# A two-branch sequence mixer: hand-ordered emission against a graph placed by a list schedule

## The chip, the cores and the metric

The kernel runs on one core of one Trainium2 chip. The metric is the device time of one execution in microseconds (us); lower is better. Each kernel was run several times on the same chip as the kernel before, and a run counts as slow when it is more than 1.5% above the fastest run of the same kernel.

Engine names: PE is the matmul engine (TensorE) and PEld its weight loads, DVE is VectorE, ACT is ScalarE, POOL is GpSimd, SP is SyncE, which issues nearly all DMAs here.

## The reference, cut to what matters

`x = A_q` is 2048 x 640 in bf16. Branch A is a long causal convolution over the sequence with a short shift convolution ahead of it; branch B is a mixer MLP; a gate per row mixes the two.

```python
def reference(A_q, A_k, A_v, A_shift_k, A_ssm_k, A_ssm_D, B_x, B_w1, B_w2, B_w3, B_w4, gate_w):
    def _A_ref(q, k, v, shift_k, ssm_k, ssm_D):
        # k_shift: 4-tap causal shift convolution of k, per column (cut)
        kv = k_shift * v
        # kv_f, kf_f: rfft of kv and of ssm_k, zero-padded to 2*S (cut)
        y_f = kv_f * kf_f[None, :, :, :]
        # y: irfft of y_f, first S rows, bf16 (cut)
        y = y + kv * ssm_D[None, None, :]
        return q * y
    def _B_ref(x, w1, w2, w3, w4):
        h = _gelu(_layernorm(x, axis=-1) @ w1)
        # hs: four column groups of h shifted by +1, -1, +2, -2 rows, then @ w2 (cut)
        x1 = x + hs
        h2 = _gelu(_layernorm(x1, axis=-1) @ w3) @ w4
        return x1 + h2
    x = A_q
    g = _sigmoid((x * gate_w).sum(-1, keepdims=True))
    # returns g * _A_ref(...) + (1 - g) * _B_ref(...)
```

## The kernel before

Sequence row `s = 16*p + t1` lies on partition `p`, slot `t1`. The Fourier transform is done in two matmul steps with an exchange between them: step 1 multiplies each of 16 slots by a table `F1` (128 x 128), the result is evacuated from PSUM into a stage `GR`, a set of 16 DMAs moves it across partitions (`gx`), step 2 multiplies by a small table `M3`. There are eight such passes: for each half of the columns (`dh`) and each half of the frequencies (`h`), one pass for the filter (`h` pass) and one for `kv`. After a `kv` pass the product with the transformed filter `HH` is multiplied back by `M3` into `VR`. An inverse for each half of the columns loads `VR` across partitions (`vx`) and multiplies by `I1`.

```python
    def gate_slab(s):                    # 16 times: product on DVE, row sum on ACT
        pr = ring.tile([P, D], BF16, name="pr", tag="xy", bufs=3)
        nc.vector.tensor_tensor(out=pr[:], in0=QX[:, s, :], in1=GW[:], op=ALU.mult)
        nc.scalar.activation(out=JK, in_=pr[:], func=ACT.Identity, accum_out=Z[:, s:s + 1])

    def step1(src, dh, h, isH, lag):
        ds = slice(dh * DH, (dh + 1) * DH)
        for tp in range(T1 // 2):
            ps = pst()
            for j in range(2):
                ...                      # F1 matmuls of slot 2*tp+j
            nc.scalar.copy(out=GR[:, 2 * tp:2 * tp + 2, :], in_=ps[:, :, 0:DH])
            yield 0.28, (lag if tp == T1 // 2 - 1 else 0.0)

    def gx_load(kp):
        gx = ring.tile([P, 2, DH], BF16, name="gx", bufs=3)
        for j in range(2):
            exchange(gx[:, j, :], GR, 2 * kp + j)        # one DMA of 80 KB, issued by SP
        return gx

    def h_step2():
        for kp in range(T1 // 2):
            gx = gx_load(kp)
            ...                          # M3 matmuls, ACT writes HH[:, ..., 0, :]
            if kp == 7:                  # HH[:, ..., 1, :] = the two partition halves swapped, 4 DMAs
                ...

    def inv(dh):
        for tp in range(T1 // 2):
            ps = pst()
            vx = ring.tile([P, 2, 2, DH], BF16, name="vx", tag="pv", bufs=3)
            for j in range(2):
                t1 = 2 * tp + j
                nc.sync.dma_start(out=vx[:, j], in_=VR.rearrange("(a r) t h d -> a r t (h d)", a=8)[:, t1])
                ...                      # 2 matmuls with I1
            ...                          # DVE: KV = ps * KV (q was loaded into KV)
            yield 0.56, 0.6

    def conv():
        for dh in range(2):
            for h in range(2):
                if (dh, h) != (0, 0):
                    yield from step1(HT, dh, h, True, LAG)       # filter pass
                    yield from h_step2()
                if (dh, h) == (1, 0):
                    q_half(0)
                    yield from inv(0)
                yield from step1(KV, dh, h, False, LAG)          # kv pass
                yield from x_step2(h, LAG if h else 0.0)
        q_half(1)
        yield from inv(1)
    # ... the front (LN, W1, W2, first filter pass) in written order, then:
    mix(cv, m2, 57.4, 86.0)              # convolution and W3/W4 work interleaved by two estimates
```

Four PSUM buffers serve all of it.

## Time and profile before

| | before |
|---|---|
| median of three runs, us | 375.05 (374.65 to 375.49) |
| span of the profiled run, us | 372.8 |
| PE busy, us; idle, us | 266.4; 106.4 |
| mean granted PE clock | 0.895 |

These are the page's lines on busy time, the span in 40 slices (each digit is the busy share, or for PEclk the granted clock, in tenths), and the chain of work that ended last, all of the kernel before. Names like R_70 are shared buffers: R_70 holds `VR`, GR the stage.

```profile
PE 266.4 (71%) x1594; PEld 151.8 (41%) x1608; DVE 186.1 (50%) x339; ACT 184.3 (49%) x280; POOL 57.0 (15%) x139
PE   0003999784697979998499998679998635634594
DVE  5326999999799985120254113231630002323286
PEclk9999999989699989999789999899999865655589
...
DVE 25%; PE 23%; DMA 22%; ACT 8%; POOL 7%; issue 7%; SPq 7%; DVEq 0%; ACTq 0%
```

No engine is full. PE is the busiest and yet idle for 106 us, so the question is where it waits. The next view sums busy time by stretches of the span of the kernel before; its columns are the stretch, its length, busy time and instruction count of each engine, the granted clock, the DMA share and the GB/s moved.

```profile
core 0: us, PE busy (x) PEld busy (x) DVE busy (x) ACT busy (x) POOL busy (x), PEclk, DMA share, GB/s
0.00:40.00 40.00, 7.56 (x42) 4.16 (x43) 19.82 (x64) 9.47 (x9) 26.98 (x76) 1.00 0.94 325
40.00:112.00 72.00, 59.51 (x431) 37.99 (x433) 68.78 (x140) 53.47 (x98) 22.69 (x56) 0.93 0.19 51
112.00:205.00 93.00, 80.50 (x492) 46.90 (x497) 46.30 (x74) 60.18 (x85) 7.34 (x9) 0.94 0.43 108
...
320.00:350.00 30.00, 12.95 (x45) 4.39 (x42) 9.68 (x12) 3.86 (x6) 0.00 (x0) 0.56 0.38 88
```

Three weak places show: the start (7.6 us of PE work in 40), the front until 112 us, in which DVE is the full engine (68.8 of 72), and the end, where the second inverse runs nearly alone at a clock of 0.56.

The gate costs DVE and ACT this much (the three groups of the kernel before, the second of which reads out the sums of the first; columns: busy us, mean ns):

```profile
L330 ACT ACTIVATE I_75<-pr 128x640 bf16<-128x640 bf16 x16 | 11.8, 735 | 3.1 <-DVE R_78 L297 2.8
L330 ACT ACTIVATION_READ_ACCUMULATOR I_75<-pr 128x1 f32 x16 | 3.0, 188 | 0.0
L329 DVE TENSOR_TENSOR pr<-QX,R_72 128x640 bf16<-128x640 bf16 x16 | 7.5, 486 | 0.4 <-ACT I_75 L330 0.4
```

### The profile page before, as it was taken

How to read it: one execution, taken by the hardware profiler on the slowest of the kernel's cores; microseconds unless marked ns; L12 is line 12 of the kernel's file. 1: busy time of each engine (PE TensorE's matmuls, PEld its weight loads, DVE VectorE, ACT ScalarE, POOL GpSimd, SP SyncE). 2: the span in 40 equal slices, each digit the busy share in tenths (PEclk: the TensorE clock that was granted, in tenths of full speed). 3: DMA queues.
4: the chain of work that ended last, by engine and by line, in shares of the span. 5: the costliest groups of instructions: out<-in, count | busy, mean ns of one | idle time of the engine just before them, and what ended most of it. 6: DMA issues, size and time to landing. Idle time of an engine off the chain costs nothing.

```text
span 372.8 us, 4494 instructions
## 1 busy us (share of the span) xinstructions
PE 266.4 (71%) x1594; PEld 151.8 (41%) x1608; DVE 186.1 (50%) x339; ACT 184.3 (49%) x280; POOL 57.0 (15%) x139
## 2 busy tenths in 40 slices
PE   0003999784697979998499998679998635634594
PEld 0002566353473545663356554235653212301163
DVE  5326999999799985120254113231630002323286
ACT  1133655689888758636367535125577644600000
POOL 3787500013674110000000000000000000000000
PEclk9999999989699989999789999899999865655589
DMA  7997400322046254047830446531402656144424
GB/s 281 409 347 269 138 0 2 127 55 53 7 101 167 56 149 138 15 110 147 206 69 20 104 110 138 130 84 33 103 10 66 142 122 199 34 100 118 117 79 150
DMA packets 47136, 43.87 MB, mean 118 GB/s; under 512 B 2319, under 2 KB 44938, under 8 KB 46986
## 3 DMA queue, kind: packets, MB, share of 16 engines
q1 hardware_dynamic: 47114, 43.59, 43.2%
q8 instruction: 12, 0.20, 0.2%
q14 instruction: 10, 0.08, 0.1%
HBM read 19.99 MB, written 2.62 MB: 61 GB/s over the span
## 4 chain that ended last, share of the span: by engine, by line
DVE 25%; PE 23%; DMA 22%; ACT 8%; POOL 7%; issue 7%; SPq 7%; DVEq 0%; ACTq 0%
DMA gx<-GR 14%; DMA vx<-R_70 6%; PE ps L509 6%; DVE R_72 L372 6%; ACT GR L400 5%; PE ps L496 5%; SPq L456 5%; POOL R_78 L170 4%; DVE R_72 L375 3%; PE ps L440 2%; DVE QX L318 2%; DVE QX L485 2%; SPq L387 2%; PE ps L441 2%; DVE pq L433 2%
## 5 line engine op out<-in xcount | busy, mean ns | idle before, releaser
L496 PE MATMUL ps<-XNT,R_76 128*128 128x512 bf16 x230 | 62.6, 393 | 1.1 <-ACT GR L400 0.3
L509 PE MATMUL ps<-R_72,R_78 128*128 128x320 bf16 x384 | 59.0, 304 | 0.3 <-ACT GR L400 0.2
L433 DVE TENSOR_TENSOR pq<-xs,R_71 128x1280 bf16<-128x1280 bf16 x32 | 26.3, 823 | 58.4 <-ACT xs L431 56.7
L509 PEld LDWEIGHTS <-R_78 128*128 128x128 bf16 x384 | 38.2, 99 | 18.6 <-issue 3.3
L400 ACT CAST GR<-ps 128x640 bf16<-128x640 f32 x64 | 39.4, 725 | 9.4 <-PE ps L397 8.9
L260 PE MATMUL pt<-IDN,xn 128*128 128x128 bf16 x160 | 14.7, 247 | 39.4 <-DVE xn L257 39.2
L500 ACT ACTIVATE R_78<-ps 128x1024 bf16<-128x1024 f32 x24 | 24.8, 1032 | 22.7 <-PE ps L496 22.7
L431 ACT CAST xs<-ps 128x640 bf16<-128x640 f32 x32 | 22.3, 695 | 27.7 <-PE ps L429 27.7
L458 PE MATMUL ps<-vx,I_75 128*128 128x320 bf16 x64 | 18.3, 387 | 23.5 <-DMA vx<-R_70 23.4
L496 PEld LDWEIGHTS <-R_76 128*128 128x128 bf16 x240 | 24.0, 101 | 25.9 <-issue 6.4
L514 DVE SCALAR_TENSOR_TENSOR QX<-ps,OMG,QX 128x640 bf16<-128x640 f32 x16 | 14.1, 883 | 40.9 <-PE ps L509 40.7
L415 ACT ACTIVATE R_71<-ps 128x640 bf16<-128x640 f32 x32 | 22.4, 700 | 23.2 <-PE ps L414 23.1
L461 DVE TENSOR_TENSOR KV<-ps,KV 128x640 bf16<-128x640 f32 x16 | 13.2, 824 | 38.1 <-PE ps L458 38.1
L260 PEld LDWEIGHTS <-xn 128*128 128x128 bf16 x160 | 12.3, 112 | 43.4 <-DVE xn L257 40.0
L429 PE MATMUL ps<-gx,M_103 128*128 128x320 bf16 x64 | 18.0, 349 | 15.5 <-DMA gx<-GR 15.3
L315 PE MATMUL ps<-R_76,R_78 128*128 128x320 bf16 x160 | 26.7, 323 | 2.3 <-issue 2.1
L442 ACT CAST R_70<-ps 128x640 bf16<-128x640 f32 x32 | 22.3, 698 | 9.7 <-PE ps L441 9.6
L257 DVE TENSOR_SCALAR xn<-QX,rs,mb 128x640 bf16<-128x640 bf16 x32 | 13.5, 438 | 26.5 <-PE pt L260 21.1
L277 PE MATMUL ps<-XNT,R_76 128*128 128x512 bf16 x96 | 24.7, 402 | 2.3 <-ACT XNT L265 2.1
L440 PE MATMUL ps<-pq,M_103 128*128 128x320 bf16 x64 | 20.6, 332 | 4.5 <-DVE pq L433 4.0
L414 PE MATMUL ps<-gx,M_103 128*128 128x320 bf16 x64 | 17.2, 304 | 8.9 <-DMA gx<-GR 8.4
L372 DVE TENSOR_TENSOR R_72<-R_70,R_72 128x1280 bf16<-128x1280 bf16 (+3 forms) x32 | 23.2, 750 | 0.0
(113 smaller groups left out, 368.3 us busy)
## 6 DMA issues: line engine op xcount, KB each, us to landing
gx<-GR SPq DMA_DIRECT2D x128, 80.0 KB
R_71<-R_71 SPq DMA_DIRECT2D x16, 320.0 KB
vx<-R_70 SPq DMA_DIRECT2D x32, 160.0 KB
R_71<-in_A_ssm_k_dram SPq DMA_DIRECT2D x5, 512.0 KB
R_70<-in_A_k_dram SPq DMA_DIRECT2D x2, 1280.0 KB
KV<-in_A_v_dram SPq DMA_DIRECT2D x1, 2560.0 KB
KV<-in_A_q_dram SPq DMA_DIRECT2D x2, 1280.0 KB
out_dram<-QX SPq DMA_DIRECT2D x16, 160.0 KB
```

The costliest lines, as they stand in the source:

```text
L260: nc.tensor.transpose(out=pt[:, j, k * P:(k + 1) * P], in_=xn[:, k * P:(k + 1) * P], identity=IDN[:])
L277: nc.tensor.matmul(ps[:, j, :], lhsT=lhsT, rhs=xt[:, k, :], start=(k == 0), stop=(k == DT - 1))
L315: nc.tensor.matmul(ps[:, j, 0:DH], lhsT=gst_ap(k, s), rhs=W2[:, k, j * DH:(j + 1) * DH], start=(k == 0), stop=(k == DT - 1))
L372: nc.vector.tensor_tensor(out=dst[:, a:b], in0=src, in1=cj, op=ALU.mult)
L400: nc.scalar.copy(out=GR[:, 2 * tp:2 * tp + 2, :], in_=ps[:, :, 0:DH])
L415: nc.scalar.activation(out=HH[:, 2 * kp:2 * kp + 2, 0, :], in_=ps[:, :, 0:DH], func=ACT.Copy, scale=1.0 / S)
L431: nc.scalar.copy(out=xs[:], in_=ps[:, :, 0:DH])
L433: nc.vector.tensor_tensor(out=pq[:], in0=xs[:].unsqueeze(2).to_broadcast([P, 2, 2, DH]), in1=HH[:, 2 * i:2 * i + 2], op=ALU.mult)
L440: nc.tensor.matmul(pv[:, j, 0:DH], lhsT=M3[:, 1, :], rhs=pq[:, j, 0, :], start=True, stop=False)
L496: nc.tensor.matmul(ps[:, j, :], lhsT=W3[:, k, (f0 + j) * P:(f0 + j + 1) * P], rhs=xt[:, k, :], start=(k == 0), stop=(k == DT - 1))
L500: nc.scalar.activation(out=GTP[:, (3 * c + f0 // 4) % 5, f0 % 4:f0 % 4 + 2, :], in_=ps[:], func=ACT.Gelu_apprx_tanh)
L509: nc.tensor.matmul(ps[:, j, 0:DH], lhsT=GTP[:, (3 * c + f // 4) % 5, f % 4, i * P:(i + 1) * P], rhs=W4[:, f, j * DH:(j + 1) * DH], start=( ...
```

## The change

The intent is to let a planner decide the order. Every piece of work becomes a node with a cost per engine that may do it, its dependencies, and the buffers it takes and gives. A list schedule simulates the core with these costs, always starting the ready node with the lowest key; the nodes are then emitted in the planned order. Keys come from a table `WANTED` of hand- or search-tuned start and end values for each stage.

```diff
+class Graph:
+    def forward(self):                       # cut to the choice of the next node
+        for opts, q in queues.items():
+            es = [e for e in opts if clock[e] <= now + 1e-9]
+            if opts == "D" and len(dmas) >= 8 and dmas[-8] > now + 1e-9:
+                continue
+            if opts == "AV" and "A" not in es and len(q) + len(queues.get("A", ())) < self.spill:
+                continue                     # an evacuation goes to DVE only if ACT is busy and 2 wait
+            ...                              # lowest key whose buffers are free wins
+        if n.bytes is not None:              # all transfers share one line in the plan
+            line = max(now + 1.9, line) + n.bytes
+            fin = line + 0.7
+    def run(self):
+        for n in sorted(self.nodes, key=lambda n: n.start):
+            n.fn(n.engine)
+SPILL = 2
+WANTED = {
+    "W1.0": (337, 568), "W2": (504, 741.5), "p0.1": (-20, 674), "p0.gx": (115.5, 1589.5),
+    "p3.1": (64, 1032.5), "p4.hh": (770, 1452.5), "inv1": (550.5, 1330.5), "W3.3": (461, 634), ...
+}
@@ convolution @@
-                    yield from step1(HT, dh, h, True, LAG)
-                    yield from h_step2()
-                ...
-                yield from step1(KV, dh, h, False, LAG)
-                yield from x_step2(h, LAG if h else 0.0)
+    def pass1(r):                            # r 0..3 the filter, r 4..7 kv
+        stage = (RA, RB)[r % 2]              # two stages in place of GR
+        war = [k_gx[r - 2, k] for k in range(T1)] if r >= 2 else k_hn_free
+        ...
+            evs.append(evac(2 * DH, PSD, [t], ...))          # ACT, or DVE by the spill rule
+    def pass2(r):
+            if r < 4:                        # filter spectrum to DRAM, 4 writes of 320 KB a pass
+                    k_hd[r, kp // 2] = dma(lambda r=r, kp=kp: HD[r, :, (kp - 1) * 2 * DH:(kp + 1) * 2 * DH], ...)
+    def hh_load(r):                          # ahead of each kv pass: one straight, one swapped copy
+        for half in range(2):
+            ns = [dma(lambda ks=ks: HH[:, 0, ks, :], lambda q=q, fs=fs: HD[q, :, fs]..., P * 5120, 5120, deps)]
+            for a in (0, 64):
+                ns.append(dma(lambda a=a, ks=ks: HH[a:a + 64, 1, ks, :], ..., 64 * 5120, 5120, deps))
@@ gate @@
-        nc.vector.tensor_tensor(out=pr[:], in0=QX[:, s, :], in1=GW[:], op=ALU.mult)
-        nc.scalar.activation(out=JK, in_=pr[:], func=ACT.Identity, accum_out=Z[:, s:s + 1])
+                for i in range(4):           # 80 one-column matmuls on the normalised, transposed x
+                    for k in range(DT):
+                        nc.tensor.matmul(P32(b)[:, 1, i:i + 1], lhsT=XNT[:, xb.slot, k, i * P:(i + 1) * P],
+                                         rhs=GWC[:, k:k + 1], start=(k == 0), stop=(k == DT - 1))
+                nc.vector.tensor_tensor(out=ZN[:, cs], in0=P32(b)[:, 1, 0:4], in1=SD[:, cs], op=ALU.mult)
+                nc.vector.scalar_tensor_tensor(out=Z[:, cs], in0=MV[:, cs, 0], scalar=GS[:], in1=ZN[:, cs], ...)
@@ inverse and end @@
-            nc.vector.tensor_tensor(out=g, in0=ps[:, :, 0:DH], in1=g, op=ALU.mult)
+                    nc.vector.scalar_tensor_tensor(out=g, in0=P32(b)[:, j, 0:DH], scalar=G32[:, t1:t1 + 1], in1=g, ...)
-        nc.vector.scalar_tensor_tensor(out=QX[:, s, :], in0=KV[:, s, :], scalar=G32[:, s:s + 1], in1=QX[:, s, :], ...)
+        k_add.append(dve(2 * D, TWO, ..., lambda p=p: nc.vector.tensor_tensor(
+            out=QX[:, 2 * p:2 * p + 2, :], in0=KV[:, 2 * p:2 * p + 2, :], in1=QX[:, 2 * p:2 * p + 2, :], op=ALU.add)))
```

Not shown: the row-shift copies are made by DMA instead of DVE, and the sine tables are made by POOL, DVE and ACT together instead of mostly by POOL.

## The prediction

> **What bounds it now.** No engine is full: the page gives PE 71%, DVE 50%, ACT 49% of a 372.8 us span. The chain of waits: DVE 25%, PE 23%, DMA 22% (the exchange gx<-GR alone 14%, vx 6%), SP queue 7%. Windows show three parts:
> - 0 to 40 us, PE busy 7.6: POOL makes the sine tables (32 pieces of 0.44 us, chained to DVE and ACT); W1 starts at 35 us.
> - 40 to 280, PE busy about 34 of each 40 us. At 40 to 120 DVE is full (39.8 and 37.0 of 40); from 120 PE leads, interrupted by "step, evacuate (8 x 0.6 us on ACT alone), exchange (16 issues at 0.65 us, then 2.7 us to land), step".
> - 280 to 373: MLP work has run out, the convolution's serial end stays: PE 25.1 of 40, 12.9 of 30, 16.3 of 23. The granted clock falls to 0.73 and 0.56, and 128x320 matmuls take 0.27 us apart instead of 0.135. The Trainium skill (TensorE: Matmul & The Clock Gate, Part 1: The HAM clock gate) says an idle PE falls to half clock; the trace agrees.
>
> PE's own work: 526 thousand columns; eight 128x320 matmuls take 1.09 us in dense stretches, hence about 224 us at full clock, 235 to 245 at the clock of dense stretches (0.91 to 1.00). Some 130 us are start, end and gaps.
>
> **What changes.**
> - *Moved, the main gain:* all four h passes go before the kv passes, into the front where PE waited for DVE; two stages let the next pass's first step overlap an exchange; MLP thirds are spread to the very end, so that inverse 1 (16 vx loads at 1.35 us, PE nearly idle at 326 to 354 now) runs beside some 25 us of W3/W4 work, at a better clock.
> - *Removed:* gate products on DVE (16 x 0.49) and ACT (16 x 0.92): 22 us; shift copies on DVE 5 us; addy (16 x 0.88) becomes 8 adds of 0.81: 7 us. Table work is split over three engines.
> - *Added:* 80 one-column matmuls with weight loads (about 7 us of PE); HD writes 5.2 MB, reads 10.5 MB, in place of 5.2 MB of on-chip swaps: about 25 us of DMA time at 400 GB/s, hidden (DMA is 43% busy).
> - *Spill to DVE:* only about 20 of 170 evacuations go there; ACT stays near 195 us, DVE near 170. Not bounds.
>
> **Sum** (estimates from the durations above). Front until W3 starts: DVE has about 100 us of work: ends near 108 us (now about 130). Rest: about 320 convolution matmuls x 0.135, W3 51 us, W4 51 us, transposes and late h steps 10 us: 155 us at full clock, 163 at 0.95. A fixed order with four PSUM buffers will stall: 18%, so about 192. Tail after the last matmul about 9 us. Total 309 us.
>
> **Prediction: 309 us, range 287 to 338. Faster by over 2%: 0.96; within 2%: 0.02; slower: 0.02.**
>
> **What would show it.** PE busy share above 80%; no stretch over 10 us with PE under half busy after 40 us; mean clock above 0.93; gx and vx together under 12% of the chain; PE's or ACT's share of the chain largest; DVE nearly full from 30 to 105 us; first W3 matmul at 100 to 115 us.
>
> **What would make it wrong.** The SP queue blocking on one unready transfer and holding gx, hh and vx behind it; ACT, which does nearly all evacuations, lagging and emptying the four PSUM buffers; fixed orders waiting for each other; exchanges slowed by HD traffic; or inverse 1 still ending alone.

## More of the kernel before

PE's waits of the kernel before say what ended its idle time (columns: total us, number of waits, longest):

```profile
PE pt L260 <- DVE xn L257: 39.2, 4, 11.7
PE ps L458 <- DMA vx<-R_70: 23.4, 23, 4.1
PE ps L429 <- DMA gx<-GR: 15.3, 9, 4.7
PE ps L414 <- DMA gx<-GR: 8.4, 18, 1.1
```

So 39.2 us wait for the LayerNorms (three waits before 33 us, 31.1 in all, and one of 8.1 at 96 us, ahead of W3), 23.7 for the exchange, and 23.4 for the loads of the inverse; together 86.3 of the 106.4.

## The result and the profile after

| | before | after |
|---|---|---|
| median, us | 375.27 (374.65 to 375.95, 4 runs) | 312.97 (309.15 to 315.04, 4 runs) |
| ratio of fast runs | | 0.827 (0.821 to 0.834) |
| span of the profiled run, us | 372.8 | 312.4 |
| PE busy; idle, us | 266.4; 106.4 | 250.7; 61.7 |
| mean granted clock | 0.895 | 0.961 |
| moved by DMA, MB | 43.87 | 54.73 |
| plan's own finish time, us | | 278.4 |

A ratio is the mean time of one kernel's fast runs over that of the other kernel's fast runs of the same rounds, so it is not quite the ratio of the medians. The profiled run of the kernel after took 314.17 us and counts as slow (1.6% above the fastest, 309.15); no fast run of it was traced. Its span is therefore up to 5 us longer than a fast run's (312.4 against 307.4); where a reading could hang on that, a second kernel with the same order is named.

The lines of the kernel after that answer to the page lines above:

```profile
PE 250.7 (80%) x1690; PEld 153.5 (49%) x1690; DVE 181.0 (58%) x343; ACT 182.2 (58%) x261; POOL 45.9 (15%) x127
PE   0297788889969896989959799965879999977845
DVE  7899779969876899341313553211358145336733
PEclk9997999999997999999989999996999999999987
...
PE 38%; DMA 27%; SPq 10%; ACT 10%; DVE 8%; issue 5%; POOL 1%; ACTq 0%; DVEq 0%
```

The span fell by 60.4 us: PE is idle 44.7 us less, and the same matmuls plus 82 more (weight loads: 1690 against 1608; the trace of before lacks 14 matmul records) take 15.7 us less, which goes with the granted clock: the row of 9s now runs to the end. The stretches of the kernel after (columns as before):

```profile
0.00:40.00 40.00, 21.42 (x186) 14.42 (x187) 34.20 (x99) 31.48 (x40) 24.78 (x74) 0.96 0.90 322
40.00:112.00 72.00, 63.84 (x494) 39.89 (x494) 60.28 (x116) 54.53 (x89) 21.11 (x53) 0.98 0.49 130
112.00:205.00 93.00, 81.74 (x501) 48.05 (x499) 39.83 (x58) 65.25 (x93) 0.00 (x0) 0.98 0.78 206
205.00:215.00 10.00, 3.19 (x18) 1.64 (x17) 0.88 (x1) 1.02 (x1) 0.00 (x0) 0.90 0.55 138
...
276.00:312.00 36.00, 23.37 (x138) 14.14 (x135) 18.66 (x29) 1.02 (x1) 0.00 (x0) 0.90 0.49 137
```

Up to 112 us PE now does 85.3 us of work (21.42 + 63.84) where it did 67.1 (7.56 + 59.51). PE's waits of the kernel after, to be set against the four lines of before:

```profile
PE ps_85 L580 <- DVE XY L572: 13.2, 3, 11.9
PE ps_87 L913 <- DMA PV<-R_71: 9.9, 4, 6.8
PE ps_88 L913 <- DMA PV<-R_71: 5.2, 3, 3.3
PE ps_86 L837 <- DMA GR<-R_72: 3.5, 3, 2.4
...
PE ps_86 L913 <- DMA PV<-R_71: 3.0, 1, 3.0
PE ps_86 L580 <- DVE XY L572: 2.9, 2, 2.0
...
PE ps_85 L913 <- DMA PV<-R_71: 1.2, 2, 1.0
...
PE ps_87 L837 <- DMA GR<-R_72: 1.0, 1, 1.0
```

The exchange is now called GR<-R_72 and the inverse's loads PV<-R_71. The wait for the LayerNorms fell from 39.2 to 16.1 us (13.2 + 2.9, all of it before 49 us), that for the exchange from 23.7 to 5.3 (the lines shown, and two of 0.5 and 0.3 left out; all of it between 54 and 93 us, in the filter passes), but that for the inverse's loads only from 23.4 to 19.3. These three sum to 45.6 us less, which is the whole 44.7 us of saved idle time within a microsecond. The largest remaining wait of the inverse, 6.81 us, is in this stretch of the timeline of the kernel after (start, us, engine, line, what; L337 is the one line that issues every DMA on SP):

```profile
209.41 0.51 SPq L337 DMA_DIRECT2D HT<-HD  x1
209.96 2.66 SPq L337 DMA_DIRECT2D PV<-R_71  x3
212.66 3.32 SPq L337 DMA_DIRECT2D HT<-HD  x3
214.55 0.69 PE L913 MATMUL ps_87<-PV,I_76 128*128 128x320 bf16 x2 [6.81 <-DMA PV<-R_71]
```

The reloads of the filter spectrum (HT<-HD) are in the same queue and on the wires at that moment. That made two suspects: SP's issuing and the reload traffic.

Milestones, read from the matmuls of each line in the two traces:

| first to last start, us | before | after |
|---|---|---|
| W1 | 35.1 to 67.6 | 25.1 to 66.4 |
| W2 | 71.7 to 111.3 | 72.0 to 105.5 |
| W3, first | 117.0 | 110.6 |
| inverses | 230.2 to 353.6 | 207.3 to 304.0 |
| last W4 | 367.7 | 308.3 |

The front became only 6.4 us shorter. What changed is what it holds: all four filter passes, where it held one.

### The profile page after: what moved, and what is told of

It reads as the page before. It is cut to its first block, busy times and chain, and to the rows that moved or that the text cites. A ratio compares the mean times of both kernels' runs of the same rounds, so it can differ in the third digit from the quotient of the medians.

```text
span 312.4 us, 4773 instructions
## 1 busy us (share of the span) xinstructions
PE 250.7 (80%) x1690; PEld 153.5 (49%) x1690; DVE 181.0 (58%) x343; ACT 182.2 (58%) x261; POOL 45.9 (15%) x127
## 2 busy tenths in 40 slices
DMA packets 41745, 54.73 MB, mean 175 GB/s; under 512 B 4986, under 2 KB 34427, under 8 KB 41722
## 3 DMA queue, kind: packets, MB, share of 16 engines
q1 hardware_dynamic: 41722, 54.44, 62.5%
## 4 chain that ended last, share of the span: by engine, by line
PE 38%; DMA 27%; SPq 10%; ACT 10%; DVE 8%; issue 5%; POOL 1%; ACTq 0%; DVEq 0%
DMA GR<-R_72 11%; SPq L337 10%; DMA PV<-R_71 8%; PE ps_86 L987 5%; ACT R_72 L327 4%; DMA R_73<-in_B_w_dram 3%; PE ps_85 L1004 3%; PE ps_85 L987 3%; DVE BST L543 2%; DMA HT<-HD 2%; PE ps_86 L1004 2%; PE ps_88 L726 2%; PE ps_87 L631 2%; PE ps_86 L726 2%; PE ps_87 L1004 1%
## 5 line engine op out<-in xcount | busy, mean ns | idle before, releaser
L1004 PEld LDWEIGHTS <-R_79 128*128 128x128 bf16 x384 | 39.1, 102 | 20.1 <-DMA R_73<-in_B_w_dram 1.5
L862 DVE TENSOR_TENSOR PV<-XS,HT 128x1280 bf16<-128x1280 bf16 x32 | 25.9, 824 | 29.5 <-ACT XS L327 27.0
L987 PEld LDWEIGHTS <-R_77 128*128 128x128 bf16 x240 | 23.3, 98 | 24.5 <-issue 4.0
L987 PE MATMUL ps_86<-XNT,R_77 128*128 128x512 bf16 x100 | 24.8, 379 | 3.6 <-ACT HST L329 3.1
L993 ACT ACTIVATE R_79<-ps_86 128x1024 bf16<-128x1024 f32 x10 | 10.2, 1023 | 25.8 <-PE ps_86 L987 20.9
L580 PEld LDWEIGHTS <-XY 128*128 128x128 bf16 x160 | 12.2, 106 | 22.1 <-DVE XY L572 17.3
L1004 PE MATMUL ps_85<-R_73,R_79 128*128 128x320 bf16 x120 | 21.0, 327 | 1.0 <-DMA R_73<-in_B_w_dram 1.0
L726 PEld LDWEIGHTS <-R_79 128*128 128x128 bf16 x160 | 16.1, 101 | 10.7 <-issue 4.3
L759 DVE TENSOR_TENSOR R_73<-R_73 128x1280 bf16<-128x1280 bf16 x24 | 19.8, 823 | 0.5
L809 PEld LDWEIGHTS <-F_75 128*128 128x128 bf16 x128 | 12.4, 100 | 15.5 <-issue 8.2
L913 PEld LDWEIGHTS <-I_76 128*128 128x128 bf16 x64 | 6.4, 103 | 25.2 <-issue 21.4
L837 PEld LDWEIGHTS <-M_95 128*128 128x128 bf16 x128 | 12.3, 98 | 10.8 <-issue 2.3
L987 PE MATMUL ps_85<-XNT,R_77 128*128 128x512 bf16 x70 | 17.4, 379 | 0.0
L1004 PE MATMUL ps_86<-R_73,R_79 128*128 128x320 bf16 x96 | 17.2, 330 | 0.0
L327 ACT CAST R_72<-ps_85 128x640 bf16<-128x640 f32 x20 | 14.1, 705 | 3.7 <-PE ps_85 L809 3.4
L631 PEld LDWEIGHTS <-R_77 128*128 128x128 bf16 x100 | 9.8, 101 | 13.1 <-issue 5.9
L1004 PE MATMUL ps_88<-R_73,R_79 128*128 128x320 bf16 x96 | 15.0, 299 | 0.0
L543 DVE BATCH_NORM_STATS2 BST<-QX 128x6 f32<-128x320 bf16 x32 | 13.7, 471 | 0.0
L737 ACT ACTIVATE I_76<-QX 128x640 bf16<-128x640 bf16 x16 | 11.8, 737 | 3.1 <-DVE QX L734 2.9
```

The source lines that it names most:

```text
L327: nc.scalar.copy(out=out(), in_=in_())
L543: nc.vector.bn_stats(out=BST[:, s % 4, j, :], in_=QX[:, s, j * DH:(j + 1) * DH])
L631: nc.tensor.matmul(P32(b)[:, j, :], lhsT=lhsT, rhs=XNT[:, xb.slot, k, :], start=(k == 0), stop=(k == DT - 1))
L726: nc.tensor.matmul(P32(b)[:, j, 0:DH], lhsT=gst_ap(k, s), rhs=W2[:, k, j * DH:(j + 1) * DH], start=(k == 0), stop=(k == DT - 1))
L759: kprev = [dve(4 * DH, TWO, kprev, lambda dst=dst: nc.vector.tensor_tensor(out=ACC[:], in0=ACC[:], in1=dst[:], op=ALU.add))]
L809: nc.tensor.matmul(P32(b)[:, j, 0:DH], lhsT=F1[:, t1, h, :], rhs=src, start=True, stop=not dt)
```

## The experiments

The theory was that the filter passes moved into the front are the main gain. The rivals were the second stage, the gate on PE, and the tuned keys themselves. Twelve kernels were run, each in one profiled and three timed rounds beside the kernel before (plain_gate_old had six runs, and its profile shows a slow one). All differences below are differences of ratios to the kernel before, times 375 us, unless medians are named. The runs were made on three chips, so only the ratios are compared across them; from their intervals a difference of two ratios is uncertain by 3 to 4 us (an estimate). "The plan's own finish" is the end that the planner in each kernel computes.

### Three undos under the tuned keys

`late_h` holds the filter passes back until the MLP's W1 or W2 is done:

```diff
-            t = ten(pe(DH, 2), deps + war, f, take=[b])
+            late = [] if r >= 4 else k_w1 if r == 0 else k_w2[-1:]
+            t = ten(pe(DH, 2), deps + war + late, f, take=[b])
```

> The changed kernel, with the h passes held back to where the kernel before had them: the first waits for the last W1 product, the other three for the last W2 product. All else (two stages, h in DRAM, gate on TensorE, evacuations, list schedule) stays. Theory (the main gain is that h work fills the front and the kv passes start early): 15 to 45 us slower than the changed kernel, that is 328 to 358 us, with the convolution's end again alone and PE under half busy in the last 30 us. Rival (the gain is the removed DVE and ACT work and the schedule, which fills gaps wherever the h passes lie): within 5 us of 313.

The edit undoes less than this text says. In the trace of late_h all four filter passes still come before the first kv pass (their first steps start from 58.6 to 144.8 us, those of kv from 162.4), whereas in the kernel before three of them lay between kv passes, until 280.3 us. It tests an early start of the filter passes, not the move out from between the kv passes.

`one_stage` takes the second stage away:

```diff
-        stage = (RA, RB)[r % 2]
-        war = [k_gx[r - 2, k] for k in range(T1)] if r >= 2 else k_hn_free
+        stage = RA
+        war = [k_gx[r - 1, k] for k in range(T1)] if r >= 1 else k_hn_free
```

> The changed kernel with one exchange stage instead of two, so the next pass's first step waits until the exchange of the pass before has read each row. Theory (two stages take the evacuations out of the exchange chain, some 5 us for each of 7 passes, but PE has other work in most of them): 5 to 20 us slower than 313. Rival (the exchange chain is not what bounds now): within 3 us.

`gate_old` puts the gate sums back on DVE and ACT:

```diff
-                        nc.tensor.matmul(P32(b)[:, 1, i:i + 1], ...)
+        k_pr.append(dve(D, TWO, [l_gw, l_q[s_]], lambda s=s_, pb=pb: nc.vector.tensor_tensor(
+            out=PR[:, pb.slot], in0=QX[:, s, :], in1=GW, op=ALU.mult), take=[pb]))
+        k_z.append(G.add({"A": (0.92, 1.0)}, [k_pr[s_]] + k_sin, lambda e, s=s_, pb=pb: nc.scalar.activation(
+            out=PR[:, pb.slot], in_=PR[:, pb.slot], func=ACT.Identity, accum_out=Z[:, s:s + 1]), give=[pb]))
...                                      # cut: a key for it; the load of W4 also waits for the products
```

> The changed kernel with the gate sums as before: 16 products on DVE (0.49 us) and 16 summing passes on ACT (0.92 us) instead of 80 one-column matmuls. Theory (only the front, where DVE is about 85 to 90% busy, pays): 3 to 10 us slower than 313. Rival one (the removed engine time counts in full): 15 to 22 us slower. Rival two (none of it is on the critical path): within 2 us.

| | median, us | ratio to before (95%) | plan's own finish, us |
|---|---|---|---|
| after | 312.97 | 0.827 (0.821 to 0.834) | 278.4 |
| late_h | 353.25 (351.60 to 353.96) | 0.939 (0.934 to 0.944) | 328.7 |
| one_stage | 353.41 (351.41 to 353.45) | 0.939 (0.934 to 0.945) | 319.0 |
| gate_old | 350.53 (348.59 to 351.67) | 0.932 (0.926 to 0.937) | 324.8 |

Each undo alone seems to cost about 40 us, and three of them would make up nearly twice the whole gain. That can't be three separate causes. The last column shows why: the planner itself already finishes 41 to 50 us later. The keys were tuned for one graph, and these three other graphs get a bad order from them: under plain keys the same edits move the plan's finish by only 3.5 to 6.4 us (next table). The undos measured the keys as much as the parts.

### The same undos under plain keys

`plain_keys` replaces the tuned table by plain consecutive stretches, written by hand once: filter pass r from 300 + 150r, kv pass r from 1000 + 500(r - 4), W3 and W4 spread over the kv passes.

```diff
-    "W1": (851, 1958.5), "W1.0": (337, 568), "W1.1": (526, 633), "W1.2": (263, 1091), "W1.3": (213.5, 699), ...
+    'W1': (100, 110), 'W1.0': (200, 260), 'W1.1': (260, 320), 'W1.2': (320, 380), 'W1.3': (380, 440), ...
```

> The changed kernel, same graph and same costs, with the tuned priorities replaced by plain ones: each stage a stretch of time in the order of the program, h passes first, kv passes and MLP thirds side by side. Theory (the graph and the early h passes give most, tuned keys the rest): 5 to 25 us slower than 313, still under 345. Rival (the gain is the tuned order): over 345.

The other three repeat the three edits above on top of it.

```diff
+            late = [] if r >= 4 else k_w1 if r == 0 else k_w2[-1:]     # plain_late_h
```

> The plain-priority kernel (323.8 us) with the h passes held back as in the run of that name with tuned priorities (which cost 40 us). Tuned priorities may suit only the graph they were tuned on. Theory (the 40 us were real: early h is the gain): 345 us or more. Rival (the tuned order was only broken by the change of graph; h passes fit anywhere as long as the schedule may re-plan): within 10 us of 324. The plan's own cost model puts it 3.5 us above the plain one.

```diff
+        stage = RA                                                      # plain_one_stage
```

> The plain-priority kernel (323.8 us) with one exchange stage. Theory (the second stage is what took exchange and evacuation off the chain): 345 us or more. Rival (the tuned order was broken): 326 to 336; the plan's cost model says 6.4 us above the plain one.

```diff
+WANTED = {'gatep': (300, 440), ...}    # plain_gate_old: the edit of gate_old, and a key for it
```

> The plain-priority kernel (323.8 us) with the gate sums on DVE and ACT as before the change. Theory (only DVE's share in the front counts, 16 x 0.49 us, and part of ACT's): 3 to 12 us above 324. Rival (the full 37 us seen with tuned priorities): 350 or more. The plan's cost model says 4.9 us above the plain one.

| | median, us | ratio to before (95%) | plan's own finish, us |
|---|---|---|---|
| plain_keys | 323.83 (322.05 to 326.81) | 0.864 (0.856 to 0.871) | 307.2 |
| plain_late_h | 337.64 (334.42 to 339.09) | 0.901 (0.895 to 0.907) | 310.7 |
| plain_one_stage | 340.21 (338.69 to 343.95) | 0.905 (0.898 to 0.911) | 313.6 |
| plain_gate_old | 335.48 (332.93 to 338.83) | 0.890 (0.885 to 0.895) | 312.1 |

With keys that fit no graph specially, holding the filter passes back costs 14.0 us, losing the second stage 15.4, and the old gate 9.9. So each matters, and no one of the three stands out: they lie within 6 us of each other, with an uncertainty of 3 to 4. The theory that an early start of the filter passes is the main gain falls; what their move out from between the kv passes is worth was not tested, as in plain_late_h too their first steps end before those of the kv passes start (60.4 to 122.3 us, kv from 129.1). The plan itself put the three undos at only 3.5, 6.4 and 4.9 us; the chip charged two to four times that. The graph with plain keys gains 51 us of the 65 that the ratios give for the whole change; the tuning of the keys adds 13.6 us (0.864 - 0.827). The trace of plain_late_h shows what holding back does: W1 is through at 59.7 us and W3 starts at 105.5, earlier than the 120.0 of plain_keys, but the last inverse matmul starts at 326.6 against 316.2. With plain keys the early filter passes lengthen the front and repay more than that at the end.

The plain kernel also shows what the tuned order avoids at the end. A stretch of plain_keys (columns as before):

```profile
300.00:322.00 22.00, 5.77 (x18) 2.16 (x17) 9.33 (x16) 0.00 (x0) 0.00 (x0) 0.50 0.57 162
```

The second inverse ends alone again, at half clock, as before the change; W4 was through at 286.9 us. The Trainium skill (TensorE: Matmul & The Clock Gate, Part 1: The HAM clock gate) says that an idle PE is let through at only half of its pulses; the 0.50 here, where PE is busy for 5.77 of 22 us, and the 1.00 of dense stretches agree, and the mean of 0.56 in the kernel before lies close to the half.

### Where 35 us between plan and chip go

The tuned plan finishes at 278.4 us and the chip needs 313. The theory was that the inverse's loads are late because SP issues everything in one queue: `vx_pool` lets POOL, idle after 112 us, issue them. The rival was the loads' landing.

```diff
-        return G.dma(nbytes, packet, deps, lambda: nc.sync.dma_start(out=out(), in_=in_()), **kw)
+        return G.dma(nbytes, packet, deps, lambda: (q or nc.sync).dma_start(out=out(), in_=in_()), **kw)
@@ inverse @@
+                                   vdeps + ns, q=nc.gpsimd if True else None, take=[vb] if j == 0 else [])
```

> The changed kernel with the 32 loads of the two inverses (PV<-R3) issued by POOL, idle by then, instead of SP; nothing else. Theory (the SP queue, 1.3 to 1.6 us for each of these issues and shared with gx, h loads and stores, holds the inverses back; PE sits idle near 207 to 215, 225 to 229 and 276 to 304 us for them): 5 to 12 us faster than 313. Rival one (the transfers themselves are slow, the issue time is back-pressure): within 2 us. Rival two (issuing from POOL costs more than it frees): slower.

It took 316.24 us (312.82 to 317.41), ratio 0.840 (0.833 to 0.846): no faster, by the ratios 4.6 us slower. This is the issue line of vx_pool (duration in ns, smallest/median/largest, then first and last start), its line in the list of DMA issues (KB each, median us from issue to landing) and its two main queues (packets, MB, share of the span of 16 DMA engines):

```profile
L337 POOL DMA_DIRECT2D PV<-R x32: 584/592/850, 201.6 to 297.7; - x32
...
PV<-R POOLq DMA_DIRECT2D x32, 160.0 KB, 7.5
...
q1 hardware_dynamic: 37370, 49.19, 54.8%
q0 software_dynamic: 2560, 5.26, 11.0%
```

An issue takes 0.59 us, the landing 7.5. The Trainium skill (DMA: Bandwidth & Descriptors, Issuing engines are not separate DMA queues) says that issuing from several engines saves only the issuing time, "which is usually small relative to the DMA itself"; these two numbers and a time that did not fall agree. But the edit changed two things: issued by POOL, the loads go through another queue, q0, which the kernel after doesn't have. There they take 11.0% of the engines' span, where taking them out of q1 brought that down by only 7.7 points (62.5 to 54.8). PE's waits for them fell from 19.3 to 15.8 us, and yet the whole got slower. So moving the loads off SP gained nothing; whether SP's queue alone costs time is not settled (it is 10% of the chain of the kernel after). The skill also says (Perfetto Trace Analysis, Per-instruction lifecycle: what the profiler-reported window actually captures) that the movement of the data lies outside the window shown for a DMA instruction, and the same two numbers show it: judged by the 0.59 us alone, these loads would look harmless.

`inv_hx` tests whether the three buffers of the inverse hold its loads back: the second inverse gets eight, in the space of the filter spectrum, which is free by then.

```diff
+    HX = HT.rearrange("p c t d -> p (c t d)").rearrange("p (b j h d) -> p b j h d", b=8, j=2, h=2)
+    G.pool("hx", 8)
-            vb = G.buf("pv")
+            vb = G.buf("hx" if dh else "pv")
+            VX = HX if dh else PV
```

> The changed kernel with eight buffers for the loads of the second inverse (in HT, free by then) instead of the three it shares. Theory (transfers of 4 to 10 us through three buffers hold the second inverse back, PE idles about 10 of 28 us there): 4 to 9 us faster than 313. Rival (the loads are served one after the other anyway, or the W4 work at the end is what is late): within 3 us.

It took 316.38 us (313.99 to 319.15), ratio 0.843 (0.837 to 0.849): a miss, by the ratio even 6 us slower. Buffers alone were not it.

`hd_small` takes the reload traffic away and leaves the order of all instructions as it is: each reload fetches one column block of eight. The result is wrong on purpose (the filter spectrum is mostly stale); it nevertheless passed the tolerance, because the convolution probably contributes little to the output (not checked), so it is a measurement and not a candidate.

```diff
-            ks = slice(half * 8, half * 8 + 8)
-            fs = slice(half * 8 * DH, (half + 1) * 8 * DH)
+            ks = slice(half * 8, half * 8 + 1)
+            fs = slice(half * 8 * DH, half * 8 * DH + DH)
```

> WRONG RESULT ON PURPOSE. The changed kernel with every load of h from DRAM (HT<-HD) cut to an eighth of its columns; every instruction, its order on each engine and each wait stays, only 9.2 of the 10.5 MB read are gone. Theory (the h reads are not hidden: they delay exchanges, stores and the inverse's loads that queue behind them, which the plan priced too low): 8 to 20 us faster than 313. Rival, and the prediction on record (25 us of transfer time, hidden since DMA is not full): within 3 us.

It took 300.47 us (299.46 to 302.41), ratio 0.804 (0.799 to 0.808), 8.9 us less by the ratios (12.5 by the medians, but that of the kernel after includes two slow runs). Here are two stretches of the kernel after, then the same two of hd_small:

```profile
170.00:205.00 35.00, 32.66 (x198) 19.17 (x197) 13.69 (x17) 23.73 (x35) 0.00 (x0) 1.00 0.83 201
205.00:240.00 35.00, 24.98 (x154) 14.97 (x153) 13.65 (x26) 6.93 (x8) 0.00 (x0) 0.90 0.51 128
```

```profile
170.00:205.00 35.00, 31.42 (x190) 18.33 (x188) 12.14 (x16) 21.88 (x32) 0.00 (x0) 1.00 0.51 125
205.00:240.00 35.00, 32.77 (x204) 19.62 (x203) 16.37 (x29) 13.93 (x17) 0.00 (x0) 0.95 0.36 83
```

Without the reloads the DMA share ahead of the first inverse falls from 0.83 to 0.51, the inverse's first load is issued at 193.8 us instead of 203.4, and the hole of PE in the next stretch closes (24.98 to 32.77 of 35). The state of the profiled run does not make this difference: vx_pool, with the same order and a fast profiled run, has a DMA share of 0.81 in the first of these stretches, 27.14 us of PE in the second, and its first load at 201.6 us. So the added traffic, which moves the total from 43.87 to 54.73 MB (45.56 in hd_small), is not hidden. That transfers wait for each other at a share of 0.83 is the likely reason, but no view here shows it directly.

### Pricing the plan

If transfers are slower than the plan believes, a plan with right prices should choose a better order. A calculation supports this: eight orders that had been run (the kernel after, plain_keys and their six undos), replayed with transfers 1.3 times as long, issues of 0.7 us and PE at 0.92 of its price, gave their eight medians within 3.3 us rms (the author's figure; the calculation is not on record, and repeated for this edition with the planners in the kept kernels it gives 4.3). The three factors were fitted to those medians, so this proves nothing by itself. `retuned_hx` is the test: inv_hx, the three prices, and the keys searched again under them.

```diff
-        n = self.add({"D": (0.6, 0.6)}, deps, lambda e: fn(), take, give)
-        n.bytes = -(-nbytes // packet) / 16.0 * (0.03 * -(-packet // 4096) + packet / 27000.0)
+        n = self.add({"D": (0.7, 0.7)}, deps, lambda e: fn(), take, give)
+        n.bytes = 1.3 * -(-nbytes // packet) / 16.0 * (0.03 * -(-packet // 4096) + packet / 27000.0)
-        return n * max(0.066, 0.000472 * cols)
+        return 0.92 * n * max(0.066, 0.000472 * cols)
-WANTED = {...}
+WANTED = {...}                           # searched again under these prices
```

> The kernel with eight buffers for the second inverse, and the plan's costs corrected from the eight kernels measured so far (transfers 1.3 times as long, 0.7 us for an issue, PE 0.92 of the price), priorities searched anew under them. Theory (the tuned kernel loses more to the chip than plain ones, 35 us against 17 to 27, because its order fits costs that the chip does not have): plan and chip come closer, 285 to 302 us on the chip where the plan says 282. Rival (any searched order overfits its plan): 305 or more.

It took 294.59 us (294.12 to 296.66), ratio 0.788 (0.784 to 0.792): faster than both kernels, 14.6 us less than after by the ratios (18.4 by the medians, slow runs included), with a correct result. Its plan ends at 282.1 us, so the gap between plan and chip is 12 us where it was 35, although the work and the bytes are those of the kernel after. These two gaps are under different prices. The same calculation puts both orders under both: at the old prices 278.4 us for the order of the kernel after and 294.9 for that of retuned_hx, at the new ones 314.6 and 282.1. The chip needs 313 and 294.6, so the old prices rank the two orders the wrong way round and the new ones rightly. But the new prices promised 32 us and the chip gave about half: the new search too found an order that its plan flatters, by 12 us against some 4 for the orders fitted. A second search under the old prices was not run, so how much of the gain is the prices and how much is more searching stays open. These are lines of retuned_hx: busy time, the chain, two of PE's waits, and the stretch in which the kernel after had its hole:

```profile
PE 247.4 (84%) x1690; PEld 153.1 (52%) x1690; DVE 182.2 (62%) x347; ACT 182.5 (62%) x259; POOL 47.6 (16%) x125
...
PE 51%; SPq 13%; DMA 12%; DVE 9%; ACT 8%; issue 3%; POOL 2%; DVEq 0%
```

```profile
PE ps L902 <- DMA HT<-R: 5.5, 3, 3.5
...
PE ps L902 <- DMA PV<-R: 2.6, 1, 2.6
```

```profile
205.00:215.00 10.00, 10.00 (x70) 6.20 (x69) 3.91 (x7) 4.09 (x6) 0.00 (x0) 1.00 0.48 124
```

The wait for the inverse's loads (L902, into HT for the second inverse) is 8.1 us instead of 19.3, DMA's share of the chain 12% instead of 27%. Whether the eight buffers help under the new keys was not separated from the keys; under the old keys they did not.

### The gate alone on the kernel before

`before_gate` leaves the kernel before as it is but for the gate.

```diff
+            for i in range(4):
+                for k in range(DT):
+                    nc.tensor.matmul(ps[:, 1, i:i + 1], lhsT=xt[:, k, i * P:(i + 1) * P], rhs=GWC[:, k:k + 1],
+                                     start=(k == 0), stop=(k == DT - 1))
-        nc.vector.tensor_tensor(out=pr[:], in0=QX[:, s, :], in1=GW[:], op=ALU.mult)
-        nc.scalar.activation(out=JK, in_=pr[:], func=ACT.Identity, accum_out=Z[:, s:s + 1])
```

> The kernel before the change with one part of it alone: gate sums as 80 one-column matmuls, in place of 16 products on DVE and 16 summing passes on ACT. Theory (DVE is full from 40 to 120 us there, so its 16 x 0.49 us come off, and the ACT sums just ahead of the first exchange too): 5 to 14 us faster than 375. Rival (this work filled gaps): within 3 us.

It took 371.51 us (371.14 to 372.69), ratio 0.994 (0.989 to 0.998): 2.3 us, the same within 2% and less than expected. The same part is worth 9.9 us in the new graph under plain keys. In the written order of the kernel before, the DVE time that it frees (7.5 us of products) is freed in one place; W2, for which the gate made way, ran from 77.7 to 105.4 us instead of 71.7 to 111.3, so 6 us were won there, and most of that was lost again by the end. Why it was lost was not followed up.

## Why the prediction was right or wrong

The time, 309 us with a range of 287 to 338, was right: 312.97 us, and the fastest run was 309.15.

- **Front.** Predicted: W3 starts near 108 us, 100 to 115 as the range. Measured: 110.6. But the text says "now about 130", and the kernel before started W3 at 117.0. The front got only 6.4 us shorter; it got fuller, by 18.2 us of PE work up to 112 us. The sum was right at this term because it used the absolute end of the front.
- **Rest.** Predicted about 192 us from W3 to the last matmul, as 163 us of work and 18% of stalls. Measured: 110.6 to 308.7, which is 198. From 112 to 312 us PE was busy 165.4 us. The size is right, but the reason given for the stalls was a fixed order with four PSUM buffers; the largest waits of PE in that part were transfers, 19.3 us for the inverse's loads, against 8.1 us for ACT, mostly evacuations (the exchange's 5.3 us all lie before 93 us).
- **Tail.** Predicted 9 us after the last matmul, measured 3.7 (308.7 to 312.4). This over-estimate and the under-estimate of the rest (6 us) cancel for the most part in the sum, which is luck.
- **"Moved, the main gain" was not borne out as a statement of weight.** Undone under plain keys the early start of the filter passes is worth 14.0 us, the second stage, which the prediction put in the same point, 15.4, the gate 9.9, the tuning of keys 13.6. The mechanism is real, and it is one of several of like size. These single numbers need not add up. The other parts (filter passes out from between the kv passes, 16 places in place of 3 for what the exchange delivers, evacuations on two engines, shift copies by DMA, tables on three engines, merged final adds) were never undone alone; that W1 starts at 25.1 us instead of 35.1 goes with the table work, but this was only argued.
- **The inverse at the end.** Predicted: inverse 1 beside W3/W4 work at a better clock. Shown: the clock from 276 us on is 0.90, where it was 0.56 in the comparable stretch of before, and PE's mean clock is 0.961 (predicted above 0.93).
- **"Hidden (DMA is 43% busy)" failed.** The reload traffic costs about 9 us by hd_small. A mean share over the span said nothing about the stretch from 170 to 205 us, where it was 0.83.
- **Gate size.** Predicted 22 us removed from DVE and ACT; the three groups are 22.3 us (11.8 + 3.0 + 7.5): right. Undoing it under plain keys cost 9.9 us, so the busy time saved is not the time saved.
- **Signs named in advance.** PE above 80%: 80.2%, just so. PE the largest share of the chain: 38%. Exchange and inverse loads under 12% of the chain: wrong, 11.0% + 8.4% = 19.4%. No stretch over 10 us with PE under half busy: wrong, PE is busy for 4.19 of the 11 us from 206 to 217. DVE nearly full from 30 to 105 us: 61.80 of 75, so 82%, weaker than said. Few evacuations on DVE: 16, counted in the emitted order, against some 20 predicted; and ACT 182 and DVE 181 us busy (195 and 170 predicted, off by 13 and 11; neither is the bound).
- **What could go wrong.** The first item of that list, SP's queue holding the inverse's loads, was tested by vx_pool: taking the loads off it gained nothing, though they went to another kind of queue; "exchanges slowed by HD traffic" points at the right source, the reloads, though their cost shows as a late start of the first inverse.

## What to carry to other kernels

Undo a part of a planned kernel only under priorities that were not tuned for the whole, or tune them again for each undo; otherwise the undo measures the loss of the tuning (here about 40 us for parts worth 10 to 15). Compare the plan's own finish time with the chip's: it was 17 us short with plain keys and 35 with tuned ones, which suggests a search that exploited wrong prices (a sign, not a proof: it was also 23 to 27 us short for the plain undos and 25 to 34 for the tuned ones). Correcting the prices from measured runs and searching again was worth more than either repair by hand (294.6 us against 316). Judge added transfers by the DMA share of the stretch where they run, not by the mean of the span.

## What the Trainium skill lacked or had wrong

- DMA: Bandwidth & Descriptors, Anatomy of one DMA — SWDGE (gpsimd) path: its fit of 2.0 us plus bytes over 436e3 gives an estimate of 2.4 us for a transfer of 160 KB. In vx_pool these POOL-issued transfers took 4.4, 7.5 and 10.5 us (smallest, median, largest) from issue to landing, at a DMA share of 0.65 to 0.83 in the stretches in which they ran. The page gives the fit per DMA; no page that bears on this gives the wait behind other transfers. How much of the excess is that wait, and how much the many small pieces of these transfers, the runs don't separate.
- No page read for this case has a method for pricing transfers in a planner. The plan's prices needed a factor of about 1.3 on transfers, fitted to eight kernels; under the three corrected prices the plan ranked the two searched orders as the chip does (314.6 and 282.1 us in the plan, 313 and 294.6 on the chip).
- TensorE: Matmul & The Clock Gate has the half clock of an idle PE, which these runs confirm (0.50). It notes that the first matmuls' slow phase varies from run to run, but not how much the whole time of one and the same program does: the four runs of the kernel after took 309.15 and 311.76 us at mean clocks of 0.978 and 0.972, and 314.17 and 315.04 us at 0.961 and 0.967.
